# Sums out of PSUM with later due times, transposes behind the last products, and a last copy into two tiles, in a fused attention and two-MLP kernel

## The chip, the cores and the metric

The kernel runs on one core of a Trainium2 chip. The metric is the device time of one execution in microseconds; before the change the median of three runs is 567.31 us (566.08 to 567.43). The engines are named as the profile names them: PE (TensorE, matrix products; PEld is its weight load), DVE (VectorE), ACT (ScalarE), POOL (GpSimd) and SP (SyncE, which here only issues DMAs). SBUF is the working memory, PSUM the memory into which PE writes.

## The reference

The reference is attention with soft-capped scores, followed by two MLPs without bias.

```
scores = cap * tanh(scale * q k^T / cap);  attn = softmax(scores);  x = attn v
x: 2 batches, 12 heads, 448 rows, 64 columns  ->  896 x 768
h = x @ w_in  (768 -> 2048);   g = elu(h);            x = g @ w_out  (2048 -> 768)
h = x @ w_in2 (768 -> 2048);   g = max(0.01 h, h);    out = g @ w_out2 (2048 -> 768)
```

The four weights come as 64-bit floating-point numbers and are turned to 32 bits on the chip, by integer operations on the two halves of each number.

## The kernel before

**Stages.** Attention for 12 pairs of heads (about 0 to 109 us of the profile), then for each MLP a stage `hidden` (L632) that computes the hidden activations in 16 blocks, and a stage `products` (L726) that multiplies them with `w_out`. In the first MLP `products` runs from about 228 to 333 us, in the second from about 448 to the end.

**Products by seven.** `products` does not multiply the 2x2 blocks of activations and weights in eight block products but in seven, in the order 7, 1, 6, 5, 3, 4, 2 (`PRODUCTS`, L696). Each of the seven has eight steps over k (`kt` 0 to 7). Operands that are sums or differences of blocks are formed on DVE in place (L718, tiles `w..` and `gg..`). Each operand is split in a high and a low part that PE can multiply at full speed: for the activations ACT rounds to `th` (L303) and DVE forms the rest `tl` (L306); for the weights they are `S..h` and `S..l`, one pair for two steps. The numbers in a name are MLP, product, step: `tl1.3.3` is MLP 1, product 3, step 3. One step is nine matmuls of 448 columns: three accumulators, each hi*hi, lo*hi (the one that needs `tl`) and hi*lo (the one that needs `S..l`). So in each step the second matmul waits for `tl`.

**Accumulators.** Of the three accumulators of a product, two lie in one PSUM tile `acc` (tag `sc`, two of them) and one in `acs` (tag `po`, two of them). A product therefore uses the PSUM that the product two places ahead of it used, some 15 us later.

**Sums out of PSUM.** `after` (L771) plans what follows each accumulator: for products 7 and 1 a copy by ACT (`u..`, L775), for the others additions on DVE: `u2` and `u7` (L779, L782), `c` (L788), a second `u2` for product 5 (L792). In MLP 1 a `c` is split again (`xh2`, `xl2`) as an input of the second MLP. In MLP 2 a `c` is transposed by PE in four pieces (L807) into a PSUM tile `ct` (tag `nt` for accumulators 0 and 2, tag `sm` for accumulator 1; one of each), copied to an SBUF tile `ob` by ACT or DVE and stored. For product 2, the last one, each accumulator's columns are stored by themselves, and the third accumulator's columns are copied in two halves, by ACT and by DVE (L833), and stored through ACT's and SP's DMA queues.

**What sets the order.** `Plan` (L24) is a list scheduler that runs when the kernel is built. Each piece has an engine, an assumed cost, the pieces that it comes after, and a time by which it should be done (`due`) or begin (`at`); `order()` (L73) derives from these a latest time for each piece, and lets each engine take, of the pieces that could start first, the one with the earliest latest time. The result is a fixed order of instructions for each engine. An engine executes its instructions in that order; what an instruction waits for (semaphores) is set by the tiles that it reads and writes.

**Weights.** The 64-bit weights are loaded into three buffers (tag `raw`), and converted by ACT (L555, L567) and DVE (L576, L585). The last of these on DVE (L585, the sign) sets the buffer free; SP issues the next load into it then.

Of the kernel before, what the change touches and what calls it, by code (L numbers as in the profile page):

```python
# [256 lines left out]
def block(ctx, tc, consts, q, k, v, w_in1, w_out1, w_in2, w_out2, out, bounded):  # L257
# [9 lines left out]
        out=qscale, in0=qscale, scalar1=1.0 / float(q.shape[3]) ** 0.5, scalar2=None, op0=ALU.mult  # L267
    )
    B, H, S, D = q.shape
# [5 lines left out]
    P = 128  # L275
    NC = 4
    CP = S // NC
# [3 lines left out]
    HALF = DM // 2  # L281
    K2 = KF // 4
    MS = HALF // P
# [8 lines left out]
        x=24, raw=3, wa=2, whi=3, wlo=3, w=2 * K2 * 2, g=2 * KF, tt=6, ea=2,  # L292
        sc=2, nt=1, po=2, sm=1,
    )
    plan = Plan(CAPACITY)
    V = {}

    def tl(pool, tag, name, shape, dtype=F32):
        V[name] = pools[pool].tile(shape, dtype, tag=tag, name=name, bufs=CAPACITY[tag])
        return V[name]  # L300

    def rounded(hi, x):
        nc.scalar.copy(hi, x)  # L303

    def remainder(lo, hi, x):
        nc.vector.tensor_tensor(out=lo, in0=x, in1=hi.bitcast(F32), op=SUB)  # L306
# [320 lines left out]
    def bank(where):  # L627
        return V[where[0]][:, where[1], :S]

    MM = 0.204  # L630
# [93 lines left out]
    outs = out.rearrange("(b p c) e -> b p c e", b=B, c=NC)  # L724

    def products(nm, T0):  # L726
        for j, p in enumerate(PRODUCTS):
# [40 lines left out]
            for m in range(MS):  # L768
                after(nm, p, m, where[m], T + (KF // 2) * 9 * MM - (6 * MM * (MS - 1 - m) if p == 2 else 0))

    def after(nm, p, m, acc, T):  # L771

        u = lambda i: f"u{nm}.{i}.{m}"
        if p in (7, 1):
            plan("ACT", 0.46, lambda: nc.scalar.copy(tl("x", "x", u(p), [P, S]), bank(acc)),  # L775
                 reads=[acc], writes=[u(p)], new={u(p): "x"}, due=T + 2)
            return
        if p == 6:
            plan("DVE", 0.54, lambda: nc.vector.tensor_tensor(  # L779
                out=tl("x", "x", u(2), [P, S]), in0=V[u(1)], in1=bank(acc), op=ADD),  # L780
                reads=[u(1), acc], writes=[u(2)], new={u(2): "x"}, due=T + 2)
            plan("DVE", 0.54, lambda: nc.vector.tensor_tensor(out=V[u(7)], in0=V[u(7)], in1=V[u(2)], op=ADD),  # L782
                 reads=[u(7), u(2)], writes=[u(7)], port=True, due=T + 5)
            return
        i, n, of, op = {2: (0, 0, 1, ADD), 3: (0, 1, 2, ADD), 4: (1, 0, 7, SUB), 5: (1, 1, 7, ADD)}[p]
        c = f"c{nm}.{i}{n}.{m}"
        home = "x" if p == 5 else "g"
        plan("DVE", 0.54, lambda: nc.vector.tensor_tensor(  # L788
            out=tl(home, home, c, [P, S]), in0=V[u(of)], in1=bank(acc), op=op),
            reads=[u(of), acc], writes=[c], new={c: home}, due=T + 2)  # L790
        if p == 5:
            plan("DVE", 0.54, lambda: nc.vector.tensor_tensor(out=V[u(2)], in0=V[u(2)], in1=bank(acc), op=ADD),  # L792
                 reads=[u(2), acc], writes=[u(2)], due=T + 3)
        if nm == "1":
            hi, lo = f"xh2.{n}.{3 * i + m}", f"xl2.{n}.{3 * i + m}"
            plan("ACT", 0.46, lambda: rounded(tl("x", "x", hi, [P, S], F32R), V[c]),
                 reads=[c], writes=[hi], new={hi: "x"}, due=T + 4)
            plan("DVE", 0.54, lambda: remainder(tl("x", "x", lo, [P, S], F32R), V[hi], V[c]),
                 reads=[c, hi], writes=[lo], new={lo: "x"}, port=True, due=T + 6)
            return  # L800
        pt, ob = f"ct{i}{n}{m}", f"ob{i}{n}"
        tag = ("nt", "sm")[m % 2]

        def transpose():
            t = tl("ps", tag, pt, [P, 512])
            for x in range(NC):
                nc.tensor.matmul(  # L807
                    t[:CP, x * P : (x + 1) * P], V[c][:, x * CP : (x + 1) * CP], ident,
                    is_transpose=True, start=True, stop=True,
                )  # L810

        plan("PE", 0.45, transpose, reads=[c], writes=[pt], new={pt: tag}, at=T + (1.5 if p != 2 else 0.1))

        def evacuate(engine, cs):
            if m == 0 and cs[0] == 0:
                tl("w", "raw", ob, [CP, NC, HALF])
            dst = V[ob][:, cs[0] : cs[1], m * P : (m + 1) * P]
            src = V[pt][:CP].rearrange("p (c e) -> p c e", c=NC)[:, cs[0] : cs[1]]
            if engine == "DVE":
                nc.vector.tensor_copy(dst, src)  # L820
            else:
                nc.scalar.copy(dst, src)  # L822

        def store(queue, ms, cs):
            e = slice(ms[0] * P, ms[-1] * P + P)
            queue.dma_start(
                out=outs[n, :, cs[0] : cs[1], i * HALF + e.start : i * HALF + e.stop],
                in_=V[ob][:, cs[0] : cs[1], e],
            )

        if p == 2 and m == MS - 1:

            for x, engine in enumerate(("ACT", "DVE")):  # L833
                cs = (x * 2, x * 2 + 2)
                plan(engine, 0.4, lambda engine=engine, cs=cs: evacuate(engine, cs), reads=[pt], writes=[(ob, m, x)])
                queue, by = ((nc.scalar, "ACT"), (nc.sync, "SP"))[x]
                plan(by, 0.6, lambda queue=queue, cs=cs: store(queue, [m], cs), reads=[(ob, m, x)], at=T + 3.0)
            return
        engine = "DVE" if m == 1 else "ACT"
        plan(engine, 0.65, lambda: evacuate(engine, (0, NC)), reads=[pt], writes=[(ob, m)],  # L840
             new={ob: "raw"} if m == 0 else None)
        ms = [m] if p == 2 else list(range(MS)) if m == MS - 1 else []
        if ms:
            plan("SP", 0.5, lambda: store(nc.sync, ms, (0, NC)), reads=[(ob, x) for x in ms], at=T + 3.0)
# [4 lines left out]
    for n in range(NPAIR):  # L849
        T = (n + 0.3) * TP  # L850
# [5 lines left out]
        if n == 0:  # L856
# [3 lines left out]
                writes=["unused"], new={"unused": "po"}, at=T - 0.7 * TP, att=True)  # L860
# [11 lines left out]
    for nm, w_in, w_out in (("1", w_in1, w_out1), ("2", w_in2, w_out2)):  # L872
        slabs = [(i, h, k2) for i, h in ((0, 0), (1, 0), (1, 1), (0, 1)) for k2 in range(K2)]
        for m in range(KF):
            due = T0 + m * TH - 12.0
            if nm == "1" and m < 3:

                due = min(due, T0 - 18.0 + 2.5 * m)
# [3 lines left out]
        for x, (i, h, k2) in enumerate(slabs):  # L882
            due = T0 + (x + 1) * TH if nm == "2" else TM + x * KF * TH / len(slabs)
# [47 lines left out]
```

## Time and profile before

| | |
|---|---|
| median of three runs | 567.31 us |
| the profiled execution: its time | 567.63 us |
| the profiled execution: span from first to last instruction | 565.8 us |
| mean granted clock of TensorE | 0.997 of full speed |
| PE busy | 553.5 us (98%), 2750 matmuls recorded |
| DVE busy | 479.9 us (85%) |
| ACT busy | 385.6 us (68%) |
| POOL busy | 52.5 us (9%) |

The span is what the profile shows from the first to the last instruction; the execution's time holds 1.8 us more. Some records of matmuls can be missing. A matmul's busy time (0.36 us here) overlaps that of the next one, so it is the distance between the starts of matmuls that says whether PE goes on at its pace, and not the share of busy time.

### The profile page before, as it was taken

To read this page: it belongs to the slowest core of one execution; us is meant where nothing else is said; L and a number is where in the kernel's file an instruction comes from. 1 tells how busy PE (TensorE), PEld (TensorE's weight loads), DVE (VectorE), ACT (ScalarE), POOL (GpSimd) and SP (SyncE) were. 2 spreads that over 40 slices of the span, in tenths; PEclk is the share of its full clock that TensorE was granted. 3 is DMA by queue.
4 is the path that set the end of the run, shared out by engine and by line. 5 is a ranking of instruction groups with operands and counts; after the bars stand their busy time and mean duration, and the time that the engine had idled before them with its cause. 6 is when DMAs were issued, how large, how long until landed. Compare 5 with 4: busy or idle time off the path is not lost.

```text
span 565.8 us, 7405 instructions
## 1 busy us (share of the span) xinstructions
PE 553.5 (98%) x2750; PEld 453.4 (80%) x2750; DVE 479.9 (85%) x628; ACT 385.6 (68%) x539; POOL 52.5 (9%) x32
## 2 busy tenths in 40 slices
PE   8999999999999999999999999999999999999994
PEld 5333333479999999999889999999999999989994
DVE  2599999987887999999999877887997599988662
ACT  4999999919877889856557656776775255545550
POOL 1554454500000000000000000000000000000000
PEclk9999999999999999999999999999999999999998
DMA  7833551154777667300031028676662000001112
GB/s 156 228 93 82 129 141 38 56 149 146 221 217 218 176 216 222 111 2 0 1 111 57 1 65 253 185 223 209 187 217 57 0 2 1 1 1 49 50 40 64
DMA packets 61435, 61.89 MB, mean 109 GB/s; under 512 B 23248, under 2 KB 53200, under 8 KB 61392
## 3 DMA queue, kind: packets, MB, share of 16 engines
q1 hardware_dynamic: 61120, 61.23, 38.1%
q8 instruction: 23, 0.38, 0.3%
q14 instruction: 20, 0.16, 0.1%
q10 hardware_dynamic: 240, 0.11, 0.1%
q0 software_dynamic: 32, 0.00, 0.0%
HBM read 58.59 MB, written 2.75 MB: 108 GB/s over the span
## 4 chain that ended last, share of the span: by engine, by line
PE 86%; DVE 6%; ACT 4%; POOL 1%; issue 1%; DMA 1%; DVEq 0%; ACTq 0%; POOLq 0%
PE acc L646 28%; PE acc L751 24%; PE acs L751 12%; PE po L496 3%; DVE rec L516 2%; PE sm L510 1%; PE ct L807 1%; PE ntq L343 1%; DMA firstk<-in_k_dram 1%; PE acs35.0_3687 L646 1%; PE acs9.1_1437 L646 1%; PE acs29.1_3302 L646 1%; PE acs15.0_1845 L646 1%; PE acs26.1_3112 L646 1%; PE acs12.0_1632 L646 1%
## 5 line engine op out<-in xcount | busy, mean ns | idle before, releaser
L516 DVE RECIPROCAL rec<-sm 128x448 f32<-128x448 f32 x12 | 35.4, 2947 | 2.4 <-PE sm L510 2.2
L358 DVE COPY kT<-ntk 128x448 f32<-128x448 f32 x12 | 7.4, 617 | 8.1 <-PE ntk L343 8.0
L343 PEld LDWEIGHTS ntq<-ident,nq 112*128 112x128 f32 x44 | 4.3, 141 | 9.3 <-DVE kT L358 8.7
L822 ACT COPY ob<-ct 112x512 f32<-112x512 f32 (+1 forms) x8 | 4.5, 560 | 10.5 <-PE ct L807 10.2
L343 PEld LDWEIGHTS ntk<-ident,nk 112*128 112x128 f32 x44 | 4.3, 141 | 7.4 <-issue 7.4
L354 DVE TENSOR_SCALAR qT<-ntq,qscale 128x448 f32<-128x448 f32 x12 | 8.1, 678 | 1.8 <-PE ntq L343 1.8
L343 PE MATMUL ntq<-ident,nq 112*128 112x112 f32 x44 | 6.6, 273 | 1.4 <-DVE kT L358 1.4
L524 DVE TENSOR_TENSOR xf<-po,rec 128x448 f32<-128x448 f32 x12 | 7.5, 623 | 0.4
L567 ACT ACTIVATE rawo1.00.2_972<-rawo1.00.2_972,third 128x768 int32<-128x768 uint8 x1 | 1.0, 1022 | 8.8 <-DMA rawo1.00.2_972<-in_moe_w_out_dram 8.8
L343 PE MATMUL ntk<-ident,nk 112*128 112x112 f32 x44 | 6.6, 273 | 0.0
L391 ACT ACTIVATE e0.0_155<-sc0.0_147 112x896 f32<-112x896 f32 x1 | 0.9, 917 | 5.2 <-PE sc0.0_147 L371 5.2
L675 ACT ACTIVATE ea2.14.0_3955<-acs38.0_3883 128x448 f32<-128x448 f32 x1 | 0.5, 546 | 5.4 <-PE acs38.0_3883 L646 5.4
L820 DVE COPY ob<-ct 112x512 f32<-112x512 f32 (+1 forms) x5 | 3.2, 636 | 1.1 <-ACT ob L822 0.6
L238 PE MATMUL unused<-busy 128*128 128x128 f32 x12 | 2.9, 434 | 1.1 <-DVE third L244 1.1
L303 ACT CAST th2.7.3_4004<-gg2.3.1_3278 128x448 fp32r<-128x448 f32 x1 | 0.6, 568 | 5.0 <-PE acs L751 5.0
L238 PEld LDWEIGHTS unused<-busy 128*128 128x128 f32 x12 | 2.6, 330 | 1.1 <-DVE third L244 1.1
L660 ACT ACTIVATE ea1.0.0_1062<-acc 128x448 f32<-128x448 f32 x1 | 0.5, 547 | 4.2 <-PE acc L646 4.2
L666 DVE SCALAR_TENSOR_TENSOR gg1.0.0_1074<-ea1.0.0_1062,acc 128x448 f32<-128x448 f32 x1 | 0.6, 620 | 3.3 <-ACT ea1.0.0_1062 L663 3.3
L788 DVE TENSOR_TENSOR c2.00.0_4963<-u2.1.0_4292,acc 128x448 f32<-128x448 f32 x1 | 0.6, 620 | 3.2 <-PE acc L751 3.2
L263 DVE TENSOR_SCALAR ncap<-capb 128x1 f32<-128x1 f32 x1 | 0.2, 153 | 3.8 <-DMA capb<-in_cap_dram 3.8
L306 DVE TENSOR_TENSOR tl2.7.3_4006<-gg2.3.1_3278,th2.7.3_4004 128x448 fp32r<-128x448 f32 x1 | 0.6, 625 | 3.0 <-ACT th2.7.3_4004 L303 3.0
L675 ACT ACTIVATE ea2.13.0_3904<-acc 128x448 f32<-128x448 f32 x1 | 0.5, 546 | 3.9 <-PE acc L646 3.9
(4974 smaller groups left out, 2265.6 us busy)
## 6 DMA issues: line engine op xcount, KB each, us to landing
nv<-in_v_dram SPq DMA_DIRECT2D x12, 224.0 KB, 3.1
nk<-in_k_dram SPq DMA_DIRECT2D x11, 224.0 KB, 3.3
nq<-in_q_dram SPq DMA_DIRECT2D x11, 224.0 KB, 3.7
out_dram<-ob SPq DMA_DIRECT2D x3, 672.0 KB, 4.4
rawg1.0_203<-in_moe_w_in_dram SPq DMA_DIRECT2D x1, 768.0 KB, 5.1
rawg1.1_248<-in_moe_w_in_dram SPq DMA_DIRECT2D x1, 768.0 KB, 5.7
rawg1.2_282<-in_moe_w_in_dram SPq DMA_DIRECT2D x1, 768.0 KB, 7.3
rawo1.00.0_514<-in_moe_w_out_dram SPq DMA_DIRECT2D x1, 768.0 KB, 5.5
```

Source lines behind the costliest of these rows:

```text
L238: nc.tensor.matmul(t, busy, busy, start=True, stop=True)
L343: nc.tensor.matmul(t[:, c * CP : (c + 1) * CP], V[f"n{nm}{n}"][:, c], ident[:CP, :CP], is_transpose=True, start=True, stop=True,)
L354: nc.vector.tensor_scalar(out=t, in0=V[pt][:, :S], scalar1=qscale, scalar2=None, op0=ALU.mult)
L358: nc.vector.tensor_copy(t, V[pt][:, :S])
L496: nc.tensor.matmul(V[po][j * D : (j + 1) * D, :S], V[f"nv{n}"][:, j, c], V[e][:, c % 2, j], start=(c == 0), stop=(c == NC - 1),)
L510: nc.tensor.matmul(t[j * D : (j + 1) * D, :S], ones[:CP], V[f"s{n}.0"][:, j], start=True, stop=True,)
L516: plan("DVE", 2.97, lambda: nc.vector.reciprocal(out=tl("att", "rec", rec, [P, S]), in_=V[sm][:, :S]), reads=[sm], writes=[rec], new={rec: ...
L524: nc.vector.tensor_tensor(out=tl("att", "xf", xf, [P, S]), in0=V[po][:, :S], in1=V[f"rec{n}"], op=ALU.mult)
L646: nc.tensor.matmul(bank(where[b]), V[g + w][:, kt, :], V[f"{part}{nm}.{b}.{kt}"], start=(x == 0 and i == 0), stop=(x == KM - 1 and i == 2),)
L751: nc.tensor.matmul(bank(where[m]), V[sp][:, kt % 2, m * P : (m + 1) * P], V[tp], start=(kt == 0 and i == 0), stop=(kt == KF // 2 - 1 and i ...
L807: nc.tensor.matmul(t[:CP, x * P : (x + 1) * P], V[c][:, x * CP : (x + 1) * CP], ident, is_transpose=True, start=True, stop=True,)
L822: nc.scalar.copy(dst, src)
```

## The change

Three things are changed, all in `after`. (1) The due times of all that reads an accumulator of products 7, 1, 6, 5, 3 and 4 are 7 us later (`free = T + 7.0`); those of product 2 are as they were. (2) The transposes of product 2 have a planned time behind all its matmuls. (3) The halves of the last copy go to two SBUF tiles of their own (`ob00.0` and `ob00.2`) and no longer to two halves of one tile `ob`.

```
+        free = T if p == 2 else T + 7.0
         if p in (7, 1):
-                 reads=[acc], writes=[u(p)], new={u(p): "x"}, due=T + 2)
+                 reads=[acc], writes=[u(p)], new={u(p): "x"}, due=free + 2)
...
-            reads=[u(of), acc], writes=[c], new={c: home}, due=T + 2)
+            reads=[u(of), acc], writes=[c], new={c: home}, due=free + 2)
...
-        plan("PE", 0.45, transpose, reads=[c], writes=[pt], new={pt: tag}, at=T + (1.5 if p != 2 else 0.1))
+        plan("PE", 0.45, transpose, reads=[c], writes=[pt], new={pt: tag}, at=T + (1.5 if p != 2 else 6 * MM * (MS - 1 - m) + 0.5 + 0.5 * m))
+
+        last = p == 2 and m == MS - 1
...
         def evacuate(engine, cs):
-            if m == 0 and cs[0] == 0:
-                tl("w", "raw", ob, [CP, NC, HALF])
-            dst = V[ob][:, cs[0] : cs[1], m * P : (m + 1) * P]
+            if last:
+                dst = tl("x", "x", f"{ob}.{cs[0]}", [P, S])[:CP, : 2 * P].rearrange("p (c e) -> p c e", c=2)
+            elif m == 0:
+                dst = tl("w", "raw", ob, [CP, NC, HALF])[:, :, :P]
+            else:
+                dst = V[ob][:, :, m * P : (m + 1) * P]
```

The first place is DVE in MLP 1, from product 3 on, where product 5 has just ended: `c1.11` and `u1.2` are the six reads of product 5's accumulators, `tl1.3.3` and `tl1.3.4` belong to steps 3 and 4 of product 3. Before:

```order
L306 TENSOR_TENSOR tl1.3.2_2565<-gg1.10.1_1714,th1.3.2_2560 128x448
L585 SCALAR_TENSOR_TENSOR w2.00.0_2376<-rawo2.00.0_2021,w2.00.0_2376 128x768
L788 TENSOR_TENSOR c1.11.0_2581<-u1.7.0_2158,acc_2396 128x448
L788 TENSOR_TENSOR c1.11.1_2583<-u1.7.1_2161,acc_2396 128x448
L788 TENSOR_TENSOR c1.11.2_2596<-u1.7.2_2164,acs_2397 128x448
L792 TENSOR_TENSOR u1.2.0_2442<-u1.2.0_2442,acc_2396 128x448
L792 TENSOR_TENSOR u1.2.1_2444<-u1.2.1_2444,acc_2396 128x448
L792 TENSOR_TENSOR u1.2.2_2446<-u1.2.2_2446,acs_2397 128x448
L306 TENSOR_TENSOR tl1.3.3_2611<-gg1.11.1_1785,th1.3.3_2577 128x448
L306 TENSOR_TENSOR S1.3.2l<-w1.10.2_1331,S1.3.2h 128x768
L306 TENSOR_TENSOR tl1.3.4_2625<-gg1.12.1_1828,th1.3.4_2609 128x448
```

And the same place of the changed kernel:

```order
L306 TENSOR_TENSOR tl1.3.2_2562<-gg1.10.1_1714,th1.3.2_2559 128x448
L576 SCALAR_TENSOR_TENSOR w2.00.0_2376<-w2.00.0_2376,rawo2.00.0_2021 128x768
L790 TENSOR_TENSOR c1.11.0_2580<-u1.7.0_2166,acc_2396 128x448
L306 TENSOR_TENSOR tl1.3.3_2582<-gg1.11.1_1785,th1.3.3_2576 128x448
L306 TENSOR_TENSOR S1.3.2l<-w1.10.2_1331,S1.3.2h 128x768
L306 TENSOR_TENSOR tl1.3.4_2599<-gg1.12.1_1828,th1.3.4_2595 128x448
L790 TENSOR_TENSOR c1.11.1_2601<-u1.7.1_2177,acc_2396 128x448
L790 TENSOR_TENSOR c1.11.2_2614<-u1.7.2_2188,acs_2397 128x448
L306 TENSOR_TENSOR S1.3.3l<-w1.10.3_1403,S1.3.3h 128x768
L306 TENSOR_TENSOR tl1.3.5_2624<-gg1.13.1_1895,th1.3.5_2620 128x448
```

`tl1.3.3` stands behind one of the six reads and no longer behind all six, and the sign operation of the weight tile `w2.00.0` (L585) has left this place; it stands 20 instructions further on, behind `tl1.4.1`. In the same manner `tl1.5.4` and `tl2.5.4` now stand ahead of five instructions that read or follow product 6 (`u.2.1`, `u.2.2`, `u.7.0` to `u.7.2`), and `tl2.6.3` ahead of two sums of activations (`gg2.0.1`, `gg2.1.1`).

The second place is DVE later in MLP 1, at the end of product 4. Before:

```order
L306 TENSOR_TENSOR tl1.4.5_2783<-gg1.5.1_1366,th1.4.5_2776 128x448
L306 TENSOR_TENSOR S1.4.3l<-w1.11.3_1694,S1.4.3h 128x768
L306 TENSOR_TENSOR tl1.4.6_2800<-gg1.6.1_1432,th1.4.6_2794 128x448
L306 TENSOR_TENSOR S1.2.0l<-w1.01.0_1763,S1.2.0h 128x768
L306 TENSOR_TENSOR tl1.4.7_2826<-gg1.7.1_1506,th1.4.7_2813 128x448
```

And of the changed kernel:

```order
L306 TENSOR_TENSOR tl1.4.6_2793<-gg1.6.1_1432,th1.4.6_2787 128x448
L306 TENSOR_TENSOR S1.2.0l<-w1.01.0_1763,S1.2.0h 128x768
L576 SCALAR_TENSOR_TENSOR w2.00.1_2795<-w2.00.1_2795,rawo2.00.1_2712 128x768
L585 SCALAR_TENSOR_TENSOR w2.00.1_2795<-rawo2.00.1_2712,w2.00.1_2795 128x768
L306 TENSOR_TENSOR tl1.4.7_2825<-gg1.7.1_1506,th1.4.7_2808 128x448
```

The two DVE operations on the weight tile `w2.00.1`, which stood some 15 instructions earlier (at `tl1.4.1` and `tl1.4.2`), stand now between `S1.2.0l` and `tl1.4.7`; their load can only be issued after the sign operation of `w2.00.0`.

The third place is the end of the program, the transposes of product 2. PE before:

```order
L751 MATMUL acc_4824<-th2.2.7_4936,S2.2.3l 128x448
L807 MATMUL ct_4965<-ident,c2.00.0_4963 112x128 x4
L751 MATMUL acs_4825<-th2.2.6_4934,S2.2.3h 128x448
L751 MATMUL acs_4825<-tl2.2.6_4947,S2.2.3h 128x448
L751 MATMUL acs_4825<-th2.2.6_4934,S2.2.3l 128x448
L751 MATMUL acs_4825<-th2.2.7_4936,S2.2.3h 128x448
L751 MATMUL acs_4825<-tl2.2.7_4949,S2.2.3h 128x448
L751 MATMUL acs_4825<-th2.2.7_4936,S2.2.3l 128x448
L807 MATMUL ct_4981<-ident,c2.00.1_4970 112x128 x4
L807 MATMUL ct_4989<-ident,c2.00.2_4986 112x128 x4
```

In the changed kernel the six matmuls of the third accumulator come first, and the last rows of DVE there, with the engines that each waits for, are these (the number behind an engine's name is the semaphore's):

```order
L790 TENSOR_TENSOR c2.00.0_4963<-u2.1.0_4297,acc_4837 128x448 [waits PE_49]
L790 TENSOR_TENSOR c2.00.1_4971<-u2.1.1_4310,acc_4837 128x448
L790 TENSOR_TENSOR c2.00.2_4978<-u2.1.2_4321,acs_4838 128x448 [waits PE_49]
L827 COPY ob_4985<-ct_4980 112x4x128 [waits DMAHW4_49,PE_49]
L827 COPY ob00.2_4997<-ct_4989 112x256 [waits Activation_49]
```

All three transposes now stand behind the last matmul, in the order of the accumulators. DVE's half of the last copy has an SBUF tile of its own, and it still waits for ACT.

## Rows read from the trace of the kernel before

**Rows 1.** Busy time by stretch: length, PE, PEld, DVE, ACT, POOL, clock, DMA.

```profile
228.00:312.00 84.00, 82.81 (x408) 76.08 (x407) 83.64 (x131) 55.14 (x92) 0.00 (x0) 1.00 0.15 46
312.00:331.00 19.00, 19.00 (x95) 17.62 (x94) 15.86 (x24) 10.97 (x19) 0.00 (x0) 1.00 0.16 40
```

**Rows 2.** Timeline of PE at four steps: start, us, engine, line, operation, tiles.

```profile
280.06 0.36 PE L751 MATMUL acc<-th1.5.4_2461,S1.5.2h 128*128 128x448 f32 x1
...
280.87 0.37 PE L751 MATMUL acc<-th1.5.4_2461,S1.5.2l 128*128 128x448 f32 x1
...
293.23 0.36 PE L751 MATMUL acc<-th1.3.3_2577,S1.3.1h 128*128 128x448 f32 x1
294.65 0.47 PE L751 MATMUL acc<-tl1.3.3_2611,S1.3.1h 128*128 128x448 f32 x1 [1.06 <-DVE tl1.3.3_2611 L306]
294.96 0.36 PE L751 MATMUL acc<-th1.3.3_2577,S1.3.1l 128*128 128x448 f32 x1
...
484.25 0.36 PE L751 MATMUL acc<-th2.6.3_4300,S2.6.1h 128*128 128x448 f32 x1
...
484.89 0.36 PE L751 MATMUL acc<-th2.6.3_4300,S2.6.1l 128*128 128x448 f32 x1
...
500.90 0.37 PE L751 MATMUL acc<-th2.5.4_4454,S2.5.2h 128*128 128x448 f32 x1
...
502.22 0.37 PE L751 MATMUL acc<-th2.5.4_4454,S2.5.2l 128*128 128x448 f32 x1
```

**Rows 3.** The chain that ended last: start, us, what.

```profile
296.54 1.22 PE acc L751 x6
```

**Rows 4.** Timeline of ACT, DVE and PE, from product 3 on.

```profile
289.58 0.57 ACT L303 CAST th1.3.3_2577<-gg1.11.1_1785 128x448 fp32r<-128x448 f32 x1 [1.25 <-PE acs L751]
...
289.93 0.94 DVE L585 SCALAR_TENSOR_TENSOR w2.00.0_2376<-rawo2.00.0_2021,w2.00.0_2376 128x768 int32<-128x768 int32 x1
290.80 0.60 DVE L788 TENSOR_TENSOR c1.11.0_2581<-u1.7.0_2158,acc 128x448 f32<-128x448 f32 x1
...
293.99 0.60 DVE L306 TENSOR_TENSOR tl1.3.3_2611<-gg1.11.1_1785,th1.3.3_2577 128x448 fp32r<-128x448 f32 x1
...
314.67 0.62 DVE L306 TENSOR_TENSOR tl1.4.7_2826<-gg1.7.1_1506,th1.4.7_2813 128x448 fp32r<-128x448 f32 x1 [1.41 <-PE acs L751]
...
316.64 0.36 PE L751 MATMUL acc<-tl1.4.7_2826,S1.4.3h 128*128 128x448 f32 x1
```

**Rows 5.** All that touches the load `rawo2.00.1`: durations in ns, then starts.

```profile
L549 SPq DMA_DIRECT2D rawo2.00.1_2601<-in_moe_w_out_dram x1: 367/367/367, 290.9 to 290.9; - x1
L567 ACT ACTIVATE rawo2.00.1_2601<-rawo2.00.1_2601,third x1: 1001/1001/1001, 297.6 to 297.6; 128x768 int32<-128x768 uint8 x1
...
L576 DVE SCALAR_TENSOR_TENSOR w2.00.1_2679<-w2.00.1_2679,rawo2.00.1_2601 x1: 940/940/940, 301.4 to 301.4; 128x768 int32<-128x768 int32 x1
...
DMA to landing us min/median/max: 5.0/5.0/5.0
```

**Rows 6.** Timeline of the end.

```profile
555.47 0.36 PE L751 MATMUL acc<-th2.2.7_4936,S2.2.3l 128*128 128x448 f32 x1
...
556.54 0.65 PE L807 MATMUL ct<-ident,c2.00.0_4963 128*112 128x128 f32 x4 [0.71 <-DVE c2.00.0_4963 L788]
...
557.23 0.59 ACT L822 COPY ob<-ct 112x512 f32<-112x512 f32 x1 [6.61 <-PE ct L807]
...
559.21 0.62 PE L807 MATMUL ct<-ident,c2.00.2_4986 128*112 128x128 f32 x4 [0.37 <-DVE c2.00.2_4986 L788]
...
560.27 0.42 DVE L820 COPY ob<-ct 112x256 f32<-112x256 f32 x1 [0.61 <-ACT ob L822]
...
560.73 1.36 SPq L826 DMA_DIRECT2D out_dram<-ob  x1
```

**Rows 7.** DMA view of 557.5 to 564.5 us, 40 slices; and time to landing.

```profile
GB/s 0 0 0 0 0 0 0 0 3 187 222 219 214 258 149 193 6 0 0 41 219 208 205 208 225 272 313 135 117 143 222 278 91 56 23 6 94 0 0 0
...
out_dram<-ob SPq DMA_DIRECT2D x1, 112.0 KB, 3.3
```

More of the change, by code (lines that the diff above doesn't have):

```diff
@@ L780, in after @@
                 out=tl("x", "x", u(2), [P, S]), in0=V[u(1)], in1=bank(acc), op=ADD),
-                reads=[u(1), acc], writes=[u(2)], new={u(2): "x"}, due=T + 2)
+                reads=[u(1), acc], writes=[u(2)], new={u(2): "x"}, due=free + 2)
             plan("DVE", 0.54, lambda: nc.vector.tensor_tensor(out=V[u(7)], in0=V[u(7)], in1=V[u(2)], op=ADD),
-                 reads=[u(7), u(2)], writes=[u(7)], port=True, due=T + 5)
+                 reads=[u(7), u(2)], writes=[u(7)], port=True, due=free + 5)
             return
@@ L789, in after @@
             out=tl(home, home, c, [P, S]), in0=V[u(of)], in1=bank(acc), op=op),
-            reads=[u(of), acc], writes=[c], new={c: home}, due=T + 2)
+            reads=[u(of), acc], writes=[c], new={c: home}, due=free + 2)
         if p == 5:
             plan("DVE", 0.54, lambda: nc.vector.tensor_tensor(out=V[u(2)], in0=V[u(2)], in1=bank(acc), op=ADD),
-                 reads=[u(2), acc], writes=[u(2)], due=T + 3)
+                 reads=[u(2), acc], writes=[u(2)], due=free + 3)
         if nm == "1":
@@ L796, in after @@
             plan("ACT", 0.46, lambda: rounded(tl("x", "x", hi, [P, S], F32R), V[c]),
-                 reads=[c], writes=[hi], new={hi: "x"}, due=T + 4)
+                 reads=[c], writes=[hi], new={hi: "x"}, due=free + 4)
             plan("DVE", 0.54, lambda: remainder(tl("x", "x", lo, [P, S], F32R), V[hi], V[c]),
-                 reads=[c, hi], writes=[lo], new={lo: "x"}, port=True, due=T + 6)
+                 reads=[c, hi], writes=[lo], new={lo: "x"}, port=True, due=free + 6)
             return
@@ L825, in store @@
             e = slice(ms[0] * P, ms[-1] * P + P)
+            if last:
+                src = V[f"{ob}.{cs[0]}"][:CP, : 2 * P].rearrange("p (c e) -> p c e", c=2)
+            else:
+                src = V[ob][:, :, e]
             queue.dma_start(
-                out=outs[n, :, cs[0] : cs[1], i * HALF + e.start : i * HALF + e.stop],
-                in_=V[ob][:, cs[0] : cs[1], e],
+                out=outs[n, :, cs[0] : cs[1], i * HALF + e.start : i * HALF + e.stop], in_=src
             )
-        if p == 2 and m == MS - 1:
+        if last:
             for x, engine in enumerate(("ACT", "DVE")):
                 cs = (x * 2, x * 2 + 2)
-                plan(engine, 0.4, lambda engine=engine, cs=cs: evacuate(engine, cs), reads=[pt], writes=[(ob, m, x)])
+                plan(engine, 0.4, lambda engine=engine, cs=cs: evacuate(engine, cs), reads=[pt], writes=[f"{ob}.{cs[0]}"], new={f"{ob}.{cs[0]}": "x"})
                 queue, by = ((nc.scalar, "ACT"), (nc.sync, "SP"))[x]
-                plan(by, 0.6, lambda queue=queue, cs=cs: store(queue, [m], cs), reads=[(ob, m, x)], at=T + 3.0)
+                plan(by, 0.6, lambda queue=queue, cs=cs: store(queue, [m], cs), reads=[f"{ob}.{cs[0]}"], at=T + 3.0)
             return
```

## The prediction

> **What bounds the kernel now.** I read the busy times first, then PE's waits, then the starts of its matmuls. PE is the bound: from the second MLP stage's start to the end almost every piece of the chain is a matmul, and six of them take 1.22 us, 0.203 us from start to start [rows 3]. The number of matmuls does not change, so only places where two starts lie further apart can be won. A list of all starts behind the attention has four such places in the steps of the two `products` stages, and the end. In each of the four the second matmul of a step, the first that reads `tl`, is late, and the one behind it starts about 0.1 us late too. From the first to the third matmul of a step should be 0.405 us. It is 0.81 at `tl1.5.4`, 1.73 at `tl1.3.3`, 0.64 at `tl2.6.3` and 1.32 at `tl2.5.4` [rows 2]. So the four places lose 0.405, 1.325, 0.235 and 0.915, together 2.88 us.
>
> The reason is DVE. From 228 to 312 us it is busy for 83.64 of 84 us, from 312 to 331 for 15.86 of 19 [rows 1]: in the first part of `products` it has no time to spare, and what stands ahead of `tl` decides. At the largest stall `th1.3.3` was rounded from 289.58 to 290.15, but `tl1.3.3` began at 293.99, behind six reads of product 5's accumulators that began at 290.80 (3.19 us, 0.53 each), and the matmul that wanted it followed 0.66 us after its start [rows 2, 4].
>
> **The change, part by part.** Step 1, the order in `products`. At `tl1.3.3` the sign operation of `w2.00.0` leaves (it held DVE from 289.93 to 290.80), so `c1.11.0` begins there and `tl1.3.3` 0.53 later, at 290.46, as `th` is ready then [rows 4]. PE wants it at 293.23 + 0.20 - 0.66 = 292.77 [rows 2, 4]. That is 2.3 us to spare, and 1.325 is won. At `tl1.5.4` and `tl2.5.4` five instructions of 0.53 go behind it: 2.65 us earlier against 0.405 and 0.915 late. At `tl2.6.3` two go, 1.06 against 0.235. All four stalls go: 2.88 us.
>
> What is late next? Nothing is removed from DVE; it is moved. PE's lead at the end of product 4 is 0.405 + 1.325 = 1.73 us, and DVE, without idle time until then, must have done 1.73 us less by the time that counts. Two weight operations on `w2.00.1` (0.87 each, as the distance 289.93 to 290.80 of the same kind shows [rows 4], so 1.74) move from ahead of that point to behind `S1.2.0l`. There DVE was idle for 1.41 us before `tl1.4.7` [rows 4]. `S1.2.0l` so ends near 314.67 - 1.41 - 1.74 = 311.5, `tl1.4.7` begins near 313.3, and PE, 1.73 ahead, wants it begun by 316.64 - 1.73 - 0.66 = 314.25: about 1.0 us to spare [rows 4]. DVE may lose a few tenths waiting for product 3's accumulators to finish, so I call it 0.5. From there to 331 DVE had 3.1 us idle [rows 1], which covers the rest. The accumulators are not late: with some 15 us between two uses of the same PSUM, a read that moves by 3 to 5 us stays far ahead of the next use; if that cover went, PE would wait before the first matmul of a product.
>
> Step 2, the load behind the moved sign operation. Its buffer comes free with it, and SP issues `rawo2.00.1` then: before at 290.9, 1.0 us after the start of the sign operation, landing 5.0 later [rows 4, 5]. The sign now stands 20 DVE instructions on, four of them of 0.87 and 16 of 0.535: 12.0 us, so at about 302.0, the issue at 303.0 and the landing at 308.0. From ACT's first touch of this tile to DVE's first lay 3.8 us [rows 5], so DVE could go on at 311.8 at the latest; it gets there at 311.5. Cost 0, covered by the spare time at `tl1.4.7`; without that, whatever the load is late.
>
> Step 3, the transposes. Before, PE's last matmul of the second accumulator began at 555.47, and PE then waited until 556.54 for the sum to transpose [rows 6]. Now six matmuls of 0.203 follow at once: the last begins at 556.69, the first transpose at 556.89, 0.35 later than before. The first copy follows 0.69 later, at 557.58, and takes 0.59 [rows 6], to 558.17. The third transpose could begin when its sum is there, 1.07 after the last matmul as above, at 557.76; but it writes the PSUM tile (tag `nt`) that the first one used, and waits for that copy: 558.2 in place of 559.21. This wait takes the place of the one removed. DVE's last copy follows 1.06 after the transpose, its store 0.46 after that [rows 6]: 559.27 and 559.73 for 560.27 and 560.73. The last store is issued 1.0 us earlier.
>
> What comes of it is less sure. The store of the first accumulator now goes out 0.35 later and those behind it closer together. In the rates, bytes move from slice 10 on, then nothing for three slices of 0.175 us, 0.53 us in all, and three further slices are at 117 to 143 GB/s in place of some 215, another 0.2 [rows 7]. If the transfers are one train, the end comes 0.53 + 0.2 - 0.35 = 0.4 earlier; if each needs its 3.3 us alone [rows 7], 1.0 earlier. Two slices reach 272 and 313 GB/s where two queues move bytes together [rows 7], which neither end has right, so I take the middle, 0.7.
>
> The Trainium skill says ("Trainium Kernel Development and Optimization", Key Constraints) that DMAs of the SP, ACT and POOL queues run on the same 16 engines, and that issuing from several saves only issue time. By that rule the end would come 0.4 earlier; the 313 GB/s of the rows speak against it in part.
>
> Step 4, the split copy. DVE's half waited 0.61 us until ACT's half was done [rows 6]. The new tiles take away their common target, but the order of the changed kernel still has DVE's copy wait for ACT: both halves read one PSUM tile. I give it 0; the bounds are 0 and 0.6 earlier, which only the SP store would have.
>
> The Trainium skill's page "PSUM — Partial Sum Buffer" (PSUM bank collisions raise a hardware error) says that two engines may not access one bank on the same partitions at once, not even to read. By it the wait has to stay, and the 0.6 can't come; no run here shows a collision.
>
> The sum: 2.88 + 0.7 = 3.58. Against the profiled execution's 567.63 us that is 564.05; it is 0.32 above the median of 567.31, from which the same sum leaves 563.73. I predict 563.8 us.
>
> **The rivals.**
> 1. Part of the lead is given back. For it: after the change the spare time at `tl1.4.7` is some 0.5 to 1.0 us, and in MLP 2 the weight and activation sums that were put behind `S2.5.0l` crowd the `tl` of product 5. Against it: only stalls that did not exist before, in places of several tenths each, would do it. If half of the 2.88 comes back: 563.8 + 1.4 = 565.2.
> 2. DVE is the bound and the order doesn't matter: the change doesn't do what it says, and each stall taken away appears at a later `tl`. For it: 83.64 of 84 us. Against it: DVE's 3.1 idle microseconds right behind [rows 1], and the 1.74 us of work moved there. It would leave the end's 0.7: 567.31 - 0.7 = 566.6.
> 3. Slower: the late load. ACT executes in order, and its first touch of `rawo2.00.1` now stands ahead of the roundings that PE needs for product 4's last steps. If the load lands more than about 1 us later than the 308.0 worked out, every further microsecond is one of PE. Against it: 5.0 us measured, on DMA queues busy for 0.15 of the time [rows 1, 5]. To be slower by 0.3% it has to eat 3.58 + 1.7 us, so to take over 11 us; at 11.5 the time would be 569.2.
>
> **How the numbers follow.** This kernel's runs tell a difference of 0.3%, 1.7 us, from none; faster is below 565.6, slower above 569.0. The forecast with its own range of 562.9 to 564.6 (the end's 0.4 to 1.6, and 0.3 us between profiled and other runs) has 0.64. Rival 1, from 564.6 to 565.9, has 0.18, four fifths of it below 565.6. Rival 2, 565.9 to 567.3, has 0.10. Rival 3 has 0.03, and another 0.05 lies below 562.9. Faster: 0.64 + 0.05 + 0.14 = 0.83; same 0.14; slower 0.03. The range that leaves out no more than 0.2 goes from 562.8 to 566.0.
>
> **What would show it.** In the profile of the changed kernel no pair of starts inside a step of `products` lies over 0.3 us apart; `tl1.3.3`, `tl1.5.4`, `tl2.5.4` and `tl2.6.3` are done over 0.5 us before PE gets to them; DVE is still near 100% busy until its new operations on `w2.00.1`, and its idle time behind them is smaller by about 1.7 us. `rawo2.00.1` is issued some 12 us later than before and nobody waits for it. The first transpose follows the last matmul within 0.25 us, the third waits for ACT's copy and not for its sum, and DVE's last copy still waits for ACT. I am wrong if a stall of over 0.3 us shows at another `tl` or `S..l`, if the second MLP's stage takes up the 1.73 us, or if the stretch from the last matmul of the second accumulator to the end of the span shrinks by less than 0.4 us.

## The result and the profile after

The changed kernel takes 562.41 us (median of four runs, 562.26 to 562.54); the kernel before, measured beside it, 567.07 (four runs, 566.08 to 567.43). The ratio is 0.9913, with a 95% interval of 0.9889 to 0.9938: faster, by 4.66 us, where 3.58 was forecast, and 0.4 us below the range. The profiled execution of the changed kernel took 562.26 us, its span is 560.4 (before: 567.63 and 565.8).

Read in the order of the prediction. First PE at the four stalls, which answers to [rows 2]: timeline of PE in the changed kernel, columns as there.

```profile
278.57 0.36 PE L751 MATMUL acc<-th1.5.4_2457,S1.5.2h 128*128 128x448 f32 x1
...
278.97 0.36 PE L751 MATMUL acc<-th1.5.4_2457,S1.5.2l 128*128 128x448 f32 x1
...
291.34 0.36 PE L751 MATMUL acc<-th1.3.3_2576,S1.3.1h 128*128 128x448 f32 x1
291.54 0.37 PE L751 MATMUL acc<-tl1.3.3_2582,S1.3.1h 128*128 128x448 f32 x1
...
481.03 0.37 PE L751 MATMUL acc<-th2.6.3_4292,S2.6.1h 128*128 128x448 f32 x1
...
481.44 0.36 PE L751 MATMUL acc<-th2.6.3_4292,S2.6.1l 128*128 128x448 f32 x1
...
497.45 0.36 PE L751 MATMUL acc<-th2.5.4_4450,S2.5.2h 128*128 128x448 f32 x1
...
497.85 0.36 PE L751 MATMUL acc<-th2.5.4_4450,S2.5.2l 128*128 128x448 f32 x1
```

From the first to the third matmul of these steps it is now 0.40 or 0.41 us; no wait is left at them. The largest distance between two starts that is left inside a step of `products` is 0.29 us, at six places in MLP 2, and it is the same at these places before. Next DVE, ACT and PE from product 3 on (answers to [rows 4]) and the load (answers to [rows 5]), in the changed kernel.

```profile
288.43 0.61 DVE L790 TENSOR_TENSOR c1.11.0_2580<-u1.7.0_2166,acc 128x448 f32<-128x448 f32 x1
288.96 0.61 DVE L306 TENSOR_TENSOR tl1.3.3_2582<-gg1.11.1_1785,th1.3.3_2576 128x448 fp32r<-128x448 f32 x1
...
312.11 0.62 DVE L306 TENSOR_TENSOR tl1.4.7_2825<-gg1.7.1_1506,th1.4.7_2808 128x448 fp32r<-128x448 f32 x1
...
313.43 0.36 PE L751 MATMUL acc<-tl1.4.7_2825,S1.4.3h 128*128 128x448 f32 x1
```

```profile
L549 SPq DMA_DIRECT2D rawo2.00.1_2712<-in_moe_w_out_dram x1: 367/367/367, 301.5 to 301.5; - x1
L567 ACT ACTIVATE rawo2.00.1_2712<-rawo2.00.1_2712,third x1: 1009/1009/1009, 306.6 to 306.6; 128x768 int32<-128x768 uint8 x1
...
L576 DVE SCALAR_TENSOR_TENSOR w2.00.1_2795<-w2.00.1_2795,rawo2.00.1_2712 x1: 953/953/953, 310.2 to 310.2; 128x768 int32<-128x768 int32 x1
...
DMA to landing us min/median/max: 4.8/4.8/4.8
```

`tl1.3.3` begins at 288.96, directly behind the first of the six reads, and PE uses it 2.58 us after that start. `tl1.4.7` begins 1.32 us ahead of its use; with the 0.66 from start to use that PE needs there are 0.66 us to spare. That is not the tightest one: `tl2.5.0` begins 0.94 us ahead of its use and has 0.28 to spare. The load is issued at 301.5 by a program whose DVE is 1.49 us ahead at this point (the start of this is below), so at 303.0 on the clock of before, and nobody waits for it. DVE's busy time in the two stretches of [rows 1], shifted by about 4 us:

```profile
224.00:308.00 84.00, 84.00 (x417) 77.85 (x416) 83.48 (x131) 54.57 (x92) 0.00 (x0) 1.00 0.14 41
308.00:327.00 19.00, 19.00 (x95) 17.62 (x94) 17.87 (x28) 13.43 (x22) 0.00 (x0) 1.00 0.23 63
```

DVE is as full as before in the first stretch, and its idle time in the second fell from 3.14 to 1.13 us: the moved work went there. The end, which answers to [rows 6], and the rates from 552 to 559 us in 40 slices, which answer to [rows 7]:

```profile
551.10 0.36 PE L751 MATMUL acc<-th2.2.7_4936,S2.2.3l 128*128 128x448 f32 x1
...
552.31 0.36 PE L751 MATMUL acs<-th2.2.7_4936,S2.2.3l 128*128 128x448 f32 x1
552.51 0.60 PE L809 MATMUL ct<-ident,c2.00.0_4963 128*112 128x128 f32 x4
...
553.15 0.58 ACT L829 COPY ob<-ct 112x512 f32<-112x512 f32 x1 [6.90 <-PE ct L809]
...
553.79 0.65 PE L809 MATMUL ct<-ident,c2.00.2_4978 128*112 128x128 f32 x4 [0.24 <-ACT ob L829]
...
554.88 0.42 DVE L827 COPY ob00.2_4997<-ct 112x256 f32<-112x256 f32 x1 [0.60 <-ACT ob00.0_4995 L829]
555.33 1.12 SPq L837 DMA_DIRECT2D out_dram<-ob00.2_4997  x1
```

```profile
GB/s 0 0 0 0 0 0 0 0 0 0 0 0 0 0 0 94 0 167 193 199 193 234 261 263 231 249 272 301 266 281 240 255 214 129 70 41 15 0 94 0
...
out_dram<-ob00.2_4997 SPq DMA_DIRECT2D x1, 112.0 KB, 3.6
```

From the second accumulator's last matmul to the third transpose it is 2.69 us (before 3.74), to the last store's issue 4.23 (before 5.26), to the end of the span 9.30 (before 10.33; spans are given to 0.1 us). The bytes go without the three empty slices, at up to 301 GB/s.

Where, then, do the 5.4 us between the two spans come from? I compared the start of every matmul in both traces. At the first products the changed kernel is 1.49 us ahead, at the second accumulator's last matmul 4.37, at the end 5.4: so 1.49 in a part that the change doesn't touch, 2.88 from the four stalls, 1.03 from the end. The 1.49 arise in the first 10 us. Timeline of PE there, the kernel before:

```profile
1.06 2.93 PE L238 MATMUL unused<-busy 128*128 128x128 f32 x12 [1.06 <-DVE third L244]
...
4.55 0.98 PE L343 MATMUL ntk<-ident,firstk 112*128 112x112 f32 x4 [0.56 <-DMA firstk<-in_k_dram]
...
8.77 1.14 PE L371 MATMUL sc0.1_152<-qT,kT 64*112 64x448 f32 x4
9.84 0.60 PE L343 MATMUL ntk<-ident,nk 112*128 112x112 f32 x4
```

And of the changed kernel:

```profile
4.34 0.57 PE L343 MATMUL ntk<-ident,firstk 112*128 112x112 f32 x4 [0.35 <-DMA firstk<-in_k_dram]
...
7.47 0.92 PE L371 MATMUL sc0.1_152<-qT,kT 64*112 64x448 f32 x4
8.32 0.60 PE L343 MATMUL ntk<-ident,nk 112*128 112x112 f32 x4
```

The same four transposes take 0.98 us in one execution and 0.57 in the other; the next four of this shape take 0.60 in both. In the kernel before PE's pace rose late, after 9 us, in the changed one before 4.6; ahead of that both had done the 12 idle matmuls and stood still for 0.56 and 0.35 us. The starts of the first four transposes lie about 0.19 us apart before and about 0.10 in the changed kernel, so the pace doubles. The traces' own record of PE's clock agrees: it has the full clock (2.4 GHz) from 9.21 us on in the kernel before and from 4.25 on in the changed one. Ahead of that it has no entry, and the view of a stretch, which takes off only a recorded loss, reads a granted clock of 1.00 there too; the half pace points to the lower level, 1.2 GHz.

With the same 12 idle matmuls eleven executions were profiled, of both kernels and of variants below. The full clock is recorded from 4.25 to 4.71 us on in four of them and from 9.0 to 10.5 in seven; the first matmul of the products of MLP 1 begins at 226.28 to 226.49 us in the four and at 227.66 to 228.33 in the seven. So the late rise costs 1.2 to 2.0 us.

The Trainium skill's page "TensorE: Matmul & The Clock Gate" (What's actually happening) says that PE starts at 1.2 GHz and is let up by its recent activity, watched in a window that does not begin with the kernel; by that rule the moment of the rise is a matter of chance. The runs agree in that, with groups 1.4 to 2 us apart, but not in the size: the page gives a scatter of 0.5 us to either side, and the rises here lie up to 6.3 us apart.

### The profile page after: what moved, and what is told of

Same layout as the page of the kernel before. It is cut to its first block, busy times and chain, and to the rows that moved or that the text cites. A ratio compares the mean times of both kernels' runs of the same rounds, so it can differ in the third digit from the quotient of the medians.

```text
span 560.4 us, 7414 instructions
## 1 busy us (share of the span) xinstructions
PE 550.4 (98%) x2750; PEld 452.7 (81%) x2750; DVE 479.8 (86%) x628; ACT 385.8 (69%) x539; POOL 52.5 (9%) x32
## 4 chain that ended last, share of the span: by engine, by line
PE 87%; DVE 5%; ACT 4%; POOL 1%; issue 1%; DMA 1%; SPq 0%; ACTq 0%; POOLq 0%
PE acc L646 29%; PE acc L751 24%; PE acs L751 12%; PE po L496 3%; DVE rec L516 2%; PE sm L510 1%; PE ct L809 1%; DMA firstq<-in_q_dram 1%; PE acs15.0_1845 L646 1%; PE acs38.0_3883 L646 1%; PE acs32.1_3492 L646 1%; PE acs9.1_1437 L646 1%; PE acs35.0_3687 L646 1%; PE acs29.1_3302 L646 1%; PE acs6.1_1242 L646 1%
## 5 line engine op out<-in xcount | busy, mean ns | idle before, releaser
L829 ACT COPY ob<-ct 112x512 f32<-112x512 f32 x7 | 4.1, 587 | 7.4 <-PE ct L809 6.9
L827 DVE COPY ob<-ct 112x512 f32<-112x512 f32 x4 | 2.8, 690 | 0.7 <-PE ct L809 0.7
```

## The experiments

Two theories on the miss: (a) the change is worth about 3.6 us as worked out, and the rest comes from which runs had the early rise; (b) the change itself brings the early rise, or one of its parts is worth more than forecast. A number that recurs below is the distance between the lowest groups of runs, since both kernels' runs fall into groups.

**due_only**, the due times alone:

```
+        free = T if p == 2 else T + 7.0
-                 reads=[acc], writes=[u(p)], new={u(p): "x"}, due=T + 2)
+                 reads=[acc], writes=[u(p)], new={u(p): "x"}, due=free + 2)
...
```

> The kernel before with the later due times alone; transposes and last copy as they were. Theory (the gains are the four stalls and the end, the rest of the difference is the start of the program, which varies from run to run): the four stalls go, 2.87 us as between the two profiled executions; first matmul of the products of MLP 1 to the last matmul of the second accumulator shorter by 2.87, tail unchanged; 567.07 - 2.87 = 564.2, give or take the 1.3 us by which the runs of the kernel before differ among themselves. Rival (the 1.5 us that the changed kernel was ahead at 10 us belongs to the change): the matmul sc0.1 begins near 7.5 us and not near 8.8 in this kernel and the time is 562.7. Rival (part 1 and part 2 hang together): less than 2.5 us of the stretch's shortening.

Measured: 564.78 us, ratio 0.9948 (0.9929 to 0.9967). Its profiled execution had the late rise, `sc0.1` at 8.65, so these due times don't always bring the early one. It was 0.09 behind before at the first products and 2.79 ahead at the last: 2.88 us. The three lowest of eight runs are at 563.19 to 563.37, 2.9 below the lowest group of before, and the other five at 564.75 to 565.45. The first rival falls.

**tail_only**, the transposes' planned time alone, and **split_only**, the two tiles alone:

```
-        ... at=T + (1.5 if p != 2 else 0.1))
+        ... at=T + (1.5 if p != 2 else 6 * MM * (MS - 1 - m) + 0.5 + 0.5 * m))
```

> The kernel before with the transposes of product 2 behind the last matmuls, alone. Theory: all up to the second accumulator's last matmul as before; first transpose 0.34 later, last one 1.05 earlier, last store issue 1.03 earlier, end of span 1.0 earlier: 566.0. Rival (the stores' train, 0.4 earlier): 566.7. Rival (the split copy is what gave the end): 0 to 0.3, 567.0.

> The kernel before with the last copy into two tiles, alone. Theory: DVE's half still waits for ACT's half, because both read one PSUM tile; end of span and time unchanged, 567.1. Rival (the common SBUF tile was what made it wait): DVE's half begins beside ACT's, 0.6 us earlier: 566.5.

Measured for tail_only: 566.29 us, ratio 0.999 (0.9973 to 1.0007); the lower half of its runs lies at 565.09 to 565.82, 0.8 below the lowest group of before. The third transpose came 2.69 us after the second accumulator's last matmul, the last store's issue 4.23, as in the changed kernel, but the end 9.56: about 0.8 earlier than before and not 1.03. For split_only: 567.09, ratio 1.0 (0.9982 to 1.0018), end after 10.31 us (before 10.33). Its last copy:

```profile
560.70 0.42 DVE L827 COPY ob00.2_4997<-ct 112x256 f32<-112x256 f32 x1 [0.61 <-ACT ob00.0_4995 L829]
```

DVE waits 0.61 us for ACT, as in [rows 6], though the two write tiles of their own.

**due5_only** and **due6_only**, the due times of one product alone (`free = T + 7.0 if p == 5 else T`, and with 6), to tell what makes up the stall at `tl1.3.3`:

> The kernel before with the later due times for the reads of product 5 alone; on DVE the six reads leave the place ahead of tl1.3.3, but the sign operation of w2.00.0 stays there. Theory (a stall at a tl is the DVE time that stands ahead of it, and goes when that time goes): tl1.3.3 begins about 2.7 us earlier, its stall of 1.325 us goes whole and stays gone, the stalls at tl1.5.4 (0.405), tl2.6.3 (0.235) and tl2.5.4 (0.915) stay: the last product begins 1.3 us earlier. Rival (DVE is the bound and the stall turns up at a later tl): 0 to 0.3 earlier. Rival (it was the sign operation of w2.00.0, 0.87 us, and not the six reads): at most 0.9 earlier.

> The kernel before with the later due times for the sums of product 6 alone; on DVE five instructions leave the place ahead of tl1.5.4 and of tl2.5.4, and the sign operation of w2.00.0 (0.87 us) leaves the place ahead of tl1.3.3, where the six reads of product 5 stay. Theory: the stalls at tl1.5.4 (0.405) and tl2.5.4 (0.915) go; at tl1.3.3 DVE gets there 0.87 earlier and PE wants it 0.405 earlier, so a stall of 1.325 - 0.87 + 0.405 = 0.86 us stays; tl2.6.3 stays at 0.235; the last product begins 0.87 + 0.915 = 1.8 us earlier. Rival (DVE is the bound): 0 to 0.3 earlier.

Measured by the traces, one execution each (566.19 and 570.55 us). due5_only: from first to third matmul 0.82 at `tl1.5.4`, 0.41 at `tl1.3.3`, 0.62 at `tl2.6.3`, 1.31 at `tl2.5.4`; only the one stall is gone, and PE gained 1.32 us in MLP 1; 0.15 of it was lost again between 502 and 511 us, where the matmuls lay further apart (below), and none at another `tl`. due6_only at `tl1.3.3`:

```profile
293.39 0.36 PE L751 MATMUL acc<-th1.3.3_2576,S1.3.1h 128*128 128x448 f32 x1
293.67 0.62 DVE L306 TENSOR_TENSOR tl1.3.3_2608<-gg1.11.1_1785,th1.3.3_2576 128x448 fp32r<-128x448 f32 x1
...
294.65 0.36 PE L751 MATMUL acc<-th1.3.3_2576,S1.3.1l 128*128 128x448 f32 x1
```

From first to third it is 1.26 us, a stall of 0.855 where 0.86 was expected: the sign operation's 0.87 gone, PE's earlier wish of 0.405 added. So the stall at this place is the DVE time ahead of the `tl`, to 0.01 us, and rival 2 of the prediction (DVE is the bound, and a stall taken away comes back at a later `tl`) is refuted. `tl1.5.4` and `tl2.5.4` went as expected. `tl2.6.3` went too, which was not expected, and the last product did not begin 1.8 us earlier but 2.8 later: from about 293 to 516 us PE's matmuls lay 0.207 apart in this execution (below), so that DVE was in time and the gain was eaten.

**ct2_own_bank** and **ct2_two_banks**, to see whether the waits left at the end are worth something:

```
-        tag = ("nt", "sm")[m % 2]
+        tag = "po" if p == 2 and m == MS - 1 else ("nt", "sm")[m % 2]
```

```
+            if last:
+                t2 = tl("ps", "sc", pt2, [P, 2, 512])[:, 0]
...
+                    (t2 if last and x >= 2 else t)[:CP, x * P : (x + 1) * P], V[c][:, x * CP : (x + 1) * CP], ident,
```

> The changed kernel with the third transpose of product 2 into a PSUM tile of its own (tag po), so that it does not wait for ACT's copy of the first. Theory A (the end follows the issue of the last stores): the third transpose begins 0.41 us earlier (553.38 in place of 553.79), ACT's and DVE's last copies and both last stores too, the time falls by 0.4 from 562.4 to 562.0. Theory B (the four last stores are one train of transfers, which begins with the first accumulator's store and that isn't earlier): the stores are issued 0.4 earlier and the end is 0 to 0.1 earlier, 562.3 to 562.4.

> The changed kernel with the third transpose into two PSUM tiles (tag po for ACT's half, tag sc for DVE's). Theory A (the end follows the issue of the last stores): as with one bank of its own, and DVE's last copy doesn't wait for ACT's but follows DVE's copy of the second accumulator, at about 554.3 in place of 554.88; last store issued 0.6 earlier, time 561.8. Theory B (one train of transfers): issue 0.6 earlier, end 0 to 0.2 earlier, 562.2 to 562.4. Rival on the split copy (the SBUF tile and not PSUM makes DVE wait): DVE's half still waits for ACT's.

Measured: ratios 0.9886 (0.9848 to 0.9924) and 0.9892 (0.9857 to 0.9927); medians 562.90 and 564.19, lowest runs 562.25 and 561.99 (of the first, one run of 1933 us, unlike all others, is left aside). The waits went as expected: the third transpose 1.08 us after the last matmul in place of 1.48, and with two banks DVE's last copy followed DVE's copy of the second accumulator without idle time, at 555.98, 0.03 us ahead of the end of ACT's. So it is the common PSUM tile that makes DVE wait in the changed kernel; two SBUF tiles alone, as in split_only, don't take the wait away. Two PSUM tiles with one SBUF tile were not run. But the last store wasn't issued earlier. Timeline of the end, two banks:

```profile
555.64 0.37 ACT L834 COPY ob00.0_4995<-ct 112x256 f32<-112x256 f32 x1
...
555.98 0.41 DVE L832 COPY ob00.2_4997<-ct002b 112x256 f32<-112x256 f32 x1
556.04 0.39 ACTq L842 DMA_DIRECT2D out_dram<-ob00.0_4995  x1
...
556.22 1.51 SPq L842 DMA_DIRECT2D out_dram<-ob  x1
...
558.13 0.36 SPq L842 DMA_DIRECT2D out_dram<-ob00.2_4997  x1
```

SP's second issue, begun while ACT issued too, took 1.51 us (0.62 in the changed kernel), and the last store left 4.04 us after the last matmul in place of 3.02. Both theories miss, as the earlier issue that they share didn't come. From the second accumulator's last matmul the end came after 9.10 us (own bank) and 10.12 (two banks).

**own_bank_act_store**, the own bank and, besides, one issue taken from SP:

```
+            queue, by = (nc.scalar, "ACT") if p == 2 and m == 0 else (nc.sync, "SP")
+            plan(by, 0.5, lambda: store(queue, ms, (0, NC)), reads=[(ob, x) for x in ms], at=T + 3.0)
```

> The changed kernel with the third transpose in a PSUM tile of its own and the first accumulator's store issued by ACT in place of SP, so that SP has two stores to issue in place of three; DVE now copies its half of the last tile ahead of ACT. Theory C (in the two kernels with an own bank SP's second issue took 1.2 and 1.5 us and delayed the last store): the last stores are issued within 2.9 us of the last matmul (3.71 and 4.04 there), the end comes 0.2 to 0.6 earlier than in the changed kernel, lowest runs at 561.8 to 562.2. Rival (train of transfers): the end is within 0.2 us of the changed kernel's.

Measured: 564.16 us, ratio 0.9929 (0.9906 to 0.9953), lowest run 562.88. The last stores were issued 2.67 and 2.73 us after the last matmul, as theory C has it, but 0.06 us from each other; their issues took 1.11 and 1.05, SP's took 5.2 us to land, and the end came after 10.30 us: no gain at all. Theory C falls; in this execution an earlier issue did not bring an earlier end.

**after_again**, the changed kernel once more:

> The changed kernel once more, unchanged. Theory (PE's pace in the first 10 us doubles early in some runs and late in others, whatever the kernel, and the four runs of the changed kernel all had the early one): its times now fall into the same groups as those of the kernel before, one near 562.4 and one 1.4 to 2 us above; the distance between the lowest runs of both is 2.87 + 1.0 = 3.8. Rival (the change itself brings the early rise): nearly all runs near 562.4, while those of the kernel before spread.

Measured: 562.91 us, ratio 0.9915 (0.9887 to 0.9944). Five runs at 562.44 to 562.91, four at 564.02 to 564.58. The profiled one, 562.91, has the early rise. This is theory (a): the changed kernel has the two groups too, and its first four runs all fell into the lower one. Of 78 runs of the kernel before, 29 lie in its lowest group (566.02 to 566.67, median 566.21); of 13 of the changed kernel, 9 (median 562.44). The distance is 3.77 us. Nothing ahead of 10 us was changed, and ct2_two_banks and own_bank_act_store, which hold the whole change, were profiled with the late rise. Whether the changed kernel has the early rise more often, 9 in 13 against 29 in 78, is not settled by so few runs.

**warm7_before**, **warm9_after** and **own_bank_warm8**, the number of idle matmuls at the start (`IDLE_PRODUCTS` 7, 9 and 8 for 6), the last with the third transpose's own bank:

> The kernel before with 7 in place of 6 idle matmuls ahead of the first transposes (12 recorded pieces become 14, 0.49 us more). Theory (PE's pace falls to about half from 4.5 to 9 us in those runs in which it stood idle too long for firstk, and that costs 1.3 to 1.5 us): the idle time ahead of the first transpose falls from 0.56 to about 0.1, the first four transposes take about 0.57 us, sc0.1 begins near 7.5 and the runs lie close together near 566.0 (the fastest of the kernel before is 566.08). Rival (the pace has nothing to do with that idle time): the start is as in the kernel before or 0.3 us later, 567.1 to 567.4, with the same spread.

> The changed kernel with 9 in place of 6 idle matmuls at the start (18 recorded pieces, 1.46 us more at the slow pace), so that PE goes on without a gap until firstk and firstq have landed. Theory (a gap or too little work by 4.3 us leaves PE at the slow pace until 7 to 10 us): the pace rises ahead of the transposes in every run, the times form one group, at 562.4 to 563.5. Rival (the time of the rise is not set by this work): two groups as with 6, both later by up to 1 us.

> The changed kernel with the third transpose in a PSUM tile of its own and 8 idle matmuls at the start. Theory (with enough idle matmuls the pace rises ahead of the transposes in every run; 9 gave one group of runs, 562.8 to 563.9): one group, 0.3 to 0.5 us earlier than with 9 because PE is free sooner, and 0 to 0.2 earlier from the transpose: 562.3 to 563.4, median 562.7, below the mean of the changed kernel's two groups (563.3). Rival (8 are too few, as 7 were): two groups, the upper one at 564 or above.

Measured: with 7 in the kernel before 567.5, ratio 1.0013 (0.9993 to 1.0034), still spread from 566.22 to 571.53; its profiled execution has the full clock from 6.8 us on, though PE stood still for only 0.30. In ct2_own_bank it came at 4.7, after 0.61 us of idle time. So the idle time ahead of the transposes does not decide, and that part of the theory falls. With 9 in the changed kernel 563.18, ratio 0.9915 (0.9885 to 0.9944), and all eight runs within 562.79 to 563.86. The profiled one:

```profile
1.06 4.21 PE L238 MATMUL unused<-busy 128*128 128x128 f32 x18 [1.06 <-DVE third L244]
5.53 0.57 PE L343 MATMUL ntk<-ident,firstk 112*128 112x112 f32 x4 [0.26 <-PE unused L238]
```

The first transposes have the full pace here (full clock from 5.3 us on), and the upper group of times is gone; but `sc0.1` begins 0.78 us later than with the early rise, so that the mean (563.23) is that of after_again's nine runs (563.30). With 8: 563.24, ratio 0.9906 (0.9876 to 0.9936), 562.08 to 564.37; its profiled execution has the full clock from 6.0 us on, behind the first transposes (0.98 us again), so 8 do not bring it ahead of them in every run. None of these beats the changed kernel by more than the runs can tell.

## Why the prediction was right and wrong

**The stalls (step 1): right.** 2.88 us forecast, 2.88 measured between the traces, in the changed kernel, in due_only and in after_again alike (there from 1.44 us ahead at the first products to 4.32). The spare time at `tl1.4.7` was 0.66 us; I had worked out 1.0 and called it 0.5. At `tl1.3.3` it was 1.92 and not 2.3, since I had left out there that PE comes 0.405 earlier once the stall at `tl1.5.4` is gone; nothing hung on it.

**The late load (step 2): right.** Issue worked out for 303.0 and measured there on the clock of before, landing 4.8 us later; cost 0.

**The transposes (step 3): mechanism right, size nearly.** First transpose 0.20 us behind the last matmul, the third one waits for ACT's copy, the last store is issued 1.03 earlier (1.0 forecast). For the end I took 0.7. In the profiled executions it was 1.03; over the six kernels with the old end (10.20 to 10.45 us, mean 10.34) and the four with the new one (9.30, 9.56, 9.96, 9.38) it is 0.79. The end scatters by several tenths: the last landing takes 3.6 us in one execution and 4.2 in another, and from it to the end of the span pass 1.8 us in the profiled execution before and 1.5 in that of the changed kernel. On the mean, 0.79, it was neither the 0.4 of one train nor the 1.0 of single transfers. Which of the two mechanisms works in one execution is not shown, and that the middle between them was near is in part luck.

**The split copy (step 4): right**, 0, and for the reason given: the common PSUM tile (ct2_two_banks).

**The level from which the sum was taken: wrong, and this is the step that failed.** The sum was set off from the profiled execution's 567.63 us and from the median of 567.31, and only 0.3 us was allowed between one run and another. That term was mis-sized: the runs showed 1.2 to 2.0 us between executions with the early and with the late rise, 1.49 of it between the two profiled ones. The execution of 567.63 us had the late rise by its trace, the run of 567.31 by its time. With the early rise the kernel before would take 567.63 - 1.49 = 566.14, and its lowest group of runs has a median of 566.21; no run of this group was profiled. From there, 566.21 - 2.88 - 0.79 = 562.54, and the four runs were at 562.26 to 562.54. The missing 1 us is not a gain of one of the three parts: due_only and split_only had the late rise, tail_only the early one, and kernels with the whole change had both. It could have been seen in the profile before: four transposes of one shape took 0.98 us at 4.55 and 0.60 at 9.84, and the three runs shown spread by 1.35 us.

The rivals: nothing of the lead was given back (rival 1), DVE was not the bound (rival 2, by due5_only and due6_only), nobody waited for the load (rival 3).

## What to carry to other kernels

In a list scheduler, too early a due time for work that nobody awaits can put it ahead of an operand that is awaited. Give reads of a buffer the time of the buffer's next use: here the stalls that went were as long as worked out from what stood ahead of the late operands, to a few hundredths, and the engine had 3.1 us of idle time behind to take up the moved work. Before a sum is set off from a measured time, look whether the same instruction runs at two paces in the profile and whether the few runs shown form groups; take both kernels at the same group, and let the range hold the distance between the groups. At the end of a program an earlier issue of the last store need not be an earlier end: look at its landing too.

## What the runs showed of the hardware

- With the same 12 idle pieces at the start, PE's full clock is recorded from 4.25 to 4.71 us on in four executions and from 9.0 to 10.5 in seven. Ahead of it transposes start about 0.19 us apart, behind it about 0.10. The view of a stretch shows a granted clock of 1.00 on both sides, so the durations, or the clock's record, have to be read. The rise is worth 1.2 to 2.0 us here. With 18 idle pieces the times of all eight runs lie in one group.
- In some stretches PE's matmuls of 448 columns lie 0.207 us apart and not 0.203, also at a granted clock of 1.00. In due6_only it held from about 293 to 516 us and cost some 4 us (an estimate: 1080 starts of 0.004), in split_only from 484 to 502; tail_only, due5_only and warm7_before have one of 11 to 14 us. Three starts of due6_only:

```profile
299.81 0.37 PE L751 MATMUL acc<-th1.3.6_2643,S1.3.3h 128*128 128x448 f32 x1
300.02 0.37 PE L751 MATMUL acc<-tl1.3.6_2660,S1.3.3h 128*128 128x448 f32 x1
300.22 0.37 PE L751 MATMUL acc<-th1.3.6_2643,S1.3.3l 128*128 128x448 f32 x1
```

  DVE's operations kept their distance of 0.53, so where PE waits for DVE the loss comes back: in split_only the stall at `tl2.5.4` shrank from 1.32 to 0.99 us between first and third matmul. What sets these stretches off stays open; whether the runs of the kernel before at 569 to 571 us had long ones is not shown, as none of them was profiled.
- An issue of a DMA by SP that fell within half a microsecond of one by ACT mostly took 0.66 to 1.76 us, against 0.36 to 0.62 alone (twice, in tail_only and due5_only, 0.36 beside ACT's); ACT's own took 0.39 or 0.40 there, and 1.05 in own_bank_act_store, where SP's began 0.06 us ahead of it. The Trainium skill's page "Perfetto Trace Analysis" (DMA Instruction — HWDGE (DVE, Sync)) says that the profiled duration of such an issue holds the wait for a descriptor generator that the issuing engines share; the long issues agree, the two short ones don't, and no run here took the sharing away.
